# Taking chunks 8 to 15 through the first layers four at a time (512 columns) instead of two (256)

## The chip, the core and the metric

The program runs on one core of a Trainium2 chip. The metric is the device time of one execution in microseconds (us), as the median of several runs. Engines are named as in the profile: PE is the matmul engine (PEld its weight loads), DVE the vector engine, ACT the scalar engine, POOL the general one, SP the queue that issues most of the transfers.

## What is computed

Three stages follow one another on 3072 tokens (4 batches of 768) of 384 features (8 heads of 48):

```python
# 1: recurrent attention, one state of 48 x 48 per batch and head
cur = einsum('bhd,bhe->bhde', u * kt, vt)
y[t] = einsum('bhd,bhde->bhe', rt, state + cur)
state = wt[..., None] * state + einsum('bhd,bhe->bhde', kt, vt)
# 2: gated layers: w1, w2 are 384 x 1024, w3 1024 x 1024, w_out 1024 x 384
x2 = ((y @ w1) * (y @ w2)) @ w3 @ w_out
# 3: 8 experts, each token goes to its best two by a noisy gate on x2
out[token] += weight * (relu(x2 @ e1[e]) @ e2[e])
```

## The kernel before

**Precision.** Every large product is made of three matmuls (`mm3`, lines 181 to 184): an operand is held as a high part and a low part in a 32-bit format that the matmul takes, and high times high, high times low and low times high are summed in a PSUM bank. ACT writes the high part as a cast, DVE the low part as a subtraction.

**Stages.** First w3 and w_out are folded into one matrix of 1024 x 384, to which the 16 gate columns are joined (400 columns). Then attention and the first layers run interleaved over 24 chunks of 128 tokens (`NCH`), which make 12 groups of two (`NGRP`, counted from 0). Then come the 8 experts.

**First layers.** For group g the x of its two chunks (256 columns) lies in `xh` and `xl`. `mo_ab(g, fp, m)` (line 576) makes 256 of the 1024 features of y @ w1 (m = 0, bank `bA`) or y @ w2 (m = 1, bank `bB`): 18 matmuls of 256 columns. For m = 0 ACT copies the bank to `acs`; for m = 1 DVE multiplies `acs` by the bank into `pp`, ACT casts that to `ph`, and DVE makes `pl`. `mo_x(g, fp)` multiplies p by the folded matrix into the two banks `bX`, 12 matmuls of 400 columns, one step behind. At a group's end DVE copies the gate columns (`mo_lz`), and ACT copies the rest to `xos` and sends it off (`mo_out`).

**Attention of chunk j** goes through the steps in `STEPS`: DVE scans the decay (`pre_scan`, `fg`), ACT makes its reciprocal by Ln and Exp (`rc`), DVE refines it and forms the scaled keys and queries (`pre_rec`, `pre_k`, `pre_r`: `kt`, `rt`), POOL and DVE make the diagonal term (`rku`, `cc`), and ACT writes it in eight pieces into `am` (`pre_d`). PE makes the scores (`at_A`), DVE puts them into `am` (`at_ov`, two instructions), and PE makes y (`at_y`), from which ACT and DVE make `xh` and `xl`. For the state the scaled keys must be turned. From chunk 5 on ACT copies them to `kp` (`at_half`, a single buffer), a transfer from ACT's queue stores them in HBM (`key_halves`), and a transposing transfer from SP's queue brings them back as `kn` (`at_turn`). Then PE makes the new part of the state (`at_kv`), DVE scales it (`snew`) and ACT puts it into `S`.

**The order.** Each step has a slot; there are 12 slots to a group, and each slot holds one piece of the first layers, behind which the steps due are written. `WHEN` holds the slots of chunks 0 to 5 by hand; later chunks take `6 * j - 14 + LATE[i]`, so that one chunk of attention goes with six slots. The gate of four chunks (`gate_top`, `gate_put`) is placed by `gate_at`. DVE executes in the order in which the program is written from the start, PE from group 2 on, ACT only in the last group; before that a scheduler sets ACT's order, and SP's but for pinned transfers. Every engine takes its queue strictly in order.

Of the kernel before, what the change touches and what calls it, by code (L numbers as in the profile page):

```python
# [18 lines left out]
P = 128  # L19
# [5 lines left out]
NGRP = NCH // 2  # L25
# [28 lines left out]
ROWMAP = np.array([r for kb in PIECES for pc in kb for r in piece_rows(pc)])  # L54
TIMES = np.concatenate([np.arange(HC)[::-1], np.arange(HC, P)])
# [16 lines left out]
def tile_kernel(ctx: ExitStack, tc: tile.TileContext, dt, nat, w3t, wout, w1, w2, e1, e2, cf, ci, out):  # L72
# [61 lines left out]
    wp.tile([P, 48], F32, name="pad_w")  # L134
    W0 = [wp.tile([P, 4, XW], F32R, name=x) for x in ("W0h", "W0l")]
# [174 lines left out]
    def at_y(j):  # L310
# [189 lines left out]
    for k, slot in WLD.items():  # L500
        at(slot, load_w, *k)
    for i, fn in enumerate(STEPS):
        for j in range(NCH):
            late = 3 if j == NCH - 1 and i == 1 else 0
            at(WHEN[j][i] if j in WHEN else 6 * j - 14 + LATE[i] - late, fn, j)
# [92 lines left out]
    def low_p():  # L598

        while LOWP:  # L600
            l, p, h = LOWP.pop()
            dve.tensor_tensor(out=l, in0=p, in1=f(h), op=OP.subtract)
# [9 lines left out]
    def mo_lz(g):  # L612
        for tt in range(2):
            dve.tensor_copy(out=LZ[:, 2 * g + tt, :], in_=bX[tt][:, DM:XW])

    def mo_out(g, tts=(0, 1), pin=lambda x: x):
        for tt in tts:
            t = 2 * g + tt
# [635 lines left out]
```

## Time and profile before

| | |
|---|---|
| median of 3 runs | 883.08 us (882.89 to 884.78) |
| the profiled execution | 885.03 us, its span 883.2 us |
| mean granted clock of PE | 0.999 |
| busy share of PE, PEld, DVE, ACT, POOL | 98%, 92%, 56%, 49%, 28% |
| share of PE in the chain that ended last | 90% |

The span runs from the first to the last instruction; 1.8 us of the profiled execution lie outside it. The busy time of PE counts overlapped matmuls, so the pace of a stream of matmuls is read from the starts in a timeline. The chain that ended last is followed back from the last instruction, each step to what released it.

### The profile page before, as it was taken

The page shows a single profiled execution, that of the slowest core. Times are in us where ns is not written, and L with a number is a line of the kernel's source. Part 1 is how long each engine was busy: PE and PEld are TensorE (multiplying, and loading weights), DVE is VectorE, ACT ScalarE, POOL GpSimd, SP SyncE. Part 2 cuts the span into 40 slices and gives each one's busy share as a digit, 9 for nine tenths or more (in the row PEclk, how much of TensorE's full clock was granted, in tenths as well). Part 3 has the DMA queues.
Part 4 walks back from the last instruction along what each step waited for, and adds up shares of the span by engine and source line. Part 5 has one row for each costly group of instructions (what it writes and reads, how often), then busy time and mean ns, then how long its engine had stood idle before and what let it go on. Part 6 is the DMA issues. An engine that isn't in the chain of part 4 may idle for free.

```text
span 883.2 us, 18271 instructions
## 1 busy us (share of the span) xinstructions
PE 868.2 (98%) x7333; PEld 808.3 (92%) x7333; DVE 497.3 (56%) x1215; ACT 435.0 (49%) x876; POOL 243.9 (28%) x216
## 2 busy tenths in 40 slices
PE   8999999999999999999999999999999999999996
PEld 6789899999999999999999989899998998989896
DVE  6899875856756756765475453352534434343430
ACT  5777666566466456555454343433433344343431
POOL 2010021041141141232344343407052260613113
PEclk9999999999999999999999999999999999999999
DMA  9955399556467464433266587829368392854213
GB/s 348 390 207 208 97 128 264 134 172 191 118 202 186 133 177 128 98 120 122 69 190 130 157 252 200 210 59 239 84 181 186 93 217 63 242 121 102 27 13 48
DMA packets 123968, 139.22 MB, mean 158 GB/s; under 512 B 74977, under 2 KB 103649, under 8 KB 123873
## 3 DMA queue, kind: packets, MB, share of 16 engines
q1 hardware_dynamic: 100336, 109.58, 43.0%
q0 software_dynamic: 12160, 19.72, 11.6%
q10 hardware_dynamic: 11376, 8.65, 3.0%
q8 instruction: 59, 0.97, 0.5%
q14 instruction: 37, 0.30, 0.1%
HBM read 88.12 MB, written 36.04 MB: 141 GB/s over the span
## 4 chain that ended last, share of the span: by engine, by line
PE 90%; DVE 6%; ACT 2%; issue 1%; DMA 1%; POOL 0%; SPq 0%; POOLq 0%; DVEq 0%; ACTq 0%
PE pb L182 27%; PE pb L183 27%; PE pb L184 26%; PE pb L332 3%; PE pb L263 3%; PE pb L932 1%; PE pb L296 1%; DVE cvz L166 1%; DMA rawf<-wout 1%; DVE w3l L173 1%; ACT top L153 0%; DVE am L268 0%; DVE WAl L173 0%; DVE fg L210 0%; PE pb L412 0%
## 5 line engine op out<-in xcount | busy, mean ns | idle before, releaser
L937 POOL DMA_INDIRECT out<-ye,ti x49 | 76.7, 1565 | 225.3 <-ACT ye L927 204.8
L910 DVE SCALAR_TENSOR_TENSOR HH<-pb,HH 128x256 fp32r<-128x256 f32 (+1 forms) x128 | 71.1, 557 | 112.5 <-ACT HH L909 112.5
L182 PE MATMUL pb<-XTh,WAh 128*128 128x512 f32 (+1 forms) x384 | 131.7, 343 | 0.0
L184 PE MATMUL pb<-XTh,WAl 128*128 128x512 f32 (+1 forms) x384 | 131.4, 342 | 0.0
L183 PE MATMUL pb<-XTl,WAh 128*128 128x512 f32 (+1 forms) x384 | 131.0, 341 | 0.0
L182 PE MATMUL pb<-WBh,HH 128*128 128x384 f32 x384 | 129.3, 337 | 0.0
L184 PE MATMUL pb<-WBh,HH 128*128 128x384 f32 x384 | 128.4, 334 | 0.0
L183 PE MATMUL pb<-WBl,HH 128*128 128x384 f32 x384 | 128.4, 334 | 0.0
L909 ACT ACTIVATE HH<-pb 128x256 fp32r<-128x256 f32 (+1 forms) x128 | 62.7, 491 | 115.6 <-PE pb L184 113.4
L742 POOL DMA_INDIRECT slots<-g_sc,g_si x48 | 51.5, 1073 | 127.5 <-DVE g_si L741 71.9
L927 ACT ACTIVATE ye<-pb,ti 128x384 f32<-128x384 f32 x42 | 24.4, 582 | 124.2 <-PE pb L184 124.2
L183 PE MATMUL pb<-xl,WAh 128*128 128x256 f32 x288 | 80.9, 281 | 0.8 <-DVE xl L339 0.8
L182 PE MATMUL pb<-xh,WAh 128*128 128x256 f32 x288 | 81.5, 284 | 0.0
L183 PE MATMUL pb<-xl,WBh 128*128 128x256 f32 x288 | 81.1, 281 | 0.0
L182 PE MATMUL pb<-xh,WBh 128*128 128x256 f32 x288 | 81.0, 281 | 0.0
L184 PE MATMUL pb<-xh,WBl 128*128 128x256 f32 x288 | 81.0, 281 | 0.0
L184 PE MATMUL pb<-xh,WAl 128*128 128x256 f32 x288 | 80.8, 281 | 0.0
L183 PEld LDWEIGHTS pb<-XTl,WAh 128*128 128x128 f32 x384 | 72.3, 188 | 7.5
L184 PEld LDWEIGHTS pb<-XTh,WAl 128*128 128x128 f32 x384 | 72.2, 188 | 7.5
L182 PEld LDWEIGHTS pb<-XTh,WAh 128*128 128x128 f32 x384 | 72.0, 188 | 7.5
L182 PEld LDWEIGHTS pb<-WBh,HH 128*128 128x128 f32 x384 | 72.1, 188 | 5.0 <-ACT WAh L810 4.4
L243 POOL TENSOR_TENSOR rku<-nrk 128x384 f32<-128x384 f32 x21 | 21.3, 1012 | 196.5 <-DVE cc L250 80.8
(203 smaller groups left out, 2069.1 us busy)
## 6 DMA issues: line engine op xcount, KB each, us to landing
dtc<-dt SPq DMA_DIRECT2D x24, 772.0 KB, 5.1
raw<-e SPq DMA_DIRECT2D x18, 768.0 KB, 6.1
raww<-e SPq DMA_DIRECT2D x14, 768.0 KB, 5.0
nrk<-nat SPq DMA_DIRECT2D x24, 384.0 KB, 5.9
expert_rows<-xg SPq DMA_DIRECT2D x45, 192.0 KB, 4.4
rawf<-w3t SPq DMA_DIRECT2D x16, 512.0 KB, 7.2
nv<-nat SPq DMA_DIRECT2D x24, 256.0 KB, 4.5
out<-zeros SPq DMA_DIRECT2D x9, 576.0 KB, 3.7
```

The costliest lines, as they stand in the source:

```text
L166: dve.scalar_tensor_tensor(z, mid, 13, t, op0=OP.logical_shift_right, op1=OP.bitwise_or)
L182: pin(pe.matmul(o, wh, xh, start=start, stop=False))
L183: pe.matmul(o, wh, xl, start=False, stop=False)
L184: pe.matmul(o, wl, xh, start=False, stop=stop)
L243: on.tensor_tensor(out=t, in0=RK[j][:, :DM], in1=RK[j][:, DM:], op=OP.mult)
L263: pe.matmul(bST[hb][:, P * a:P * a + P], KT[j][q, a].rearrange("p s i -> p (s i)"), RT[j][q, a].rearrange("p s i -> p (s i)"), start=True, ...
L332: pe.matmul(o, lt, rh, start=st, stop=en, tile_position=tp)
L742: ins = pool.indirect_dma_start(out=table, out_offset=bass.IndirectOffsetOnAxis(ap=si[:, i, k:k + 1], axis=0), in_=SC[:, i, k, :], in_offs ...
L909: act.activation(out=Hh[hf][:, ff], in_=bank[:, :n], func=AF.Relu)
L910: dve.scalar_tensor_tensor(Hl[hf][:, ff], bank[:, :n], 0.0, f(Hh[hf][:, ff]), op0=OP.max, op1=OP.subtract)
L927: act.activation(out=y[:n], in_=bank[:n], func=AF.Copy, scale=wt)
L937: ins = pool.indirect_dma_start(out=out, out_offset=bass.IndirectOffsetOnAxis(ap=ti(e, j)[:, 0:1], axis=0), in_=y[:n], in_offset=None, com ...
```

## The change

Groups 4 and 5 now hold four chunks each (8 to 11 and 12 to 15), so there are 10 groups. In a group of four a `mo_ab` makes 128 features for 512 columns with 9 matmuls. p of two chunks goes straight through the second product (`mo_x4` with `tts` 0 and 1); p of the other two chunks is kept in `ps` (and `pl` for the last two features) and goes through it in a second pass, behind the first piece of the next group. Since a group of four needs four chunks of x at its start, the y of chunks 6 to 19 gets slots of its own (`YAT`): 26 instead of 28 for chunk 6, 34 instead of 40 for chunk 8, 46 instead of 58 for chunk 11, then falling back to the old pace by chunk 20. The other steps of a chunk are scaled by `f`, 4/6 where chunks follow one another by four slots. The buffers of x become one pair of tiles and one pair taken from the weight loader's pool; the gate of chunks 8 to 15 is placed later.

```diff
+GROUPS = ((0, 2, 0, 0), (2, 2, 0, 6 * P), (4, 2, 0, 0), (6, 2, 0, 6 * P), (8, 4, 1, 0), (12, 4, 0, 0),
+          (16, 2, 1, 0), (18, 2, 1, 6 * P), (20, 2, 0, 0), (22, 2, 0, 6 * P))
...
+    YAT = {4: 16, 5: 22, 6: 26, 7: 30, 8: 34, 9: 38, 10: 42, 11: 46, 12: 52, 13: 58, 14: 64, 15: 70, 16: 80, 17: 90,
+           18: 98, 19: 106}
+
+    def when(j, i):
+        if j in WHEN:
+            return WHEN[j][i]
+        base, y, f = 6 * j - 14, 6 * j - 8, 1
+        if j < 21:
+            base = YAT[j - 1]
+            y, f = YAT.get(j, y), min(1, (base - YAT[j - 2]) / 6)
+        return y - 3 * (j == NCH - 1 and i == 1) if LATE[i] == 6 else base + f * LATE[i]
...
-            at(WHEN[j][i] if j in WHEN else 6 * j - 14 + LATE[i] - late, fn, j)
+            at(when(j, i), fn, j)
...
+        if GROUPS[g][1] == 4:
+            for kb in range(3):
+                o = 768 * (fp // 2) + 256 * kb + P * (fp % 2)
+                mm3(bank, wh[:, o:o + P], wl[:, o:o + P], XH[g][:, kb], XL[g][:, kb], kb == 0, kb == 2)
...
+    def mo_p(g, fp):
+        p = PP[g, fp]
+        if GROUPS[g][1] == 4:
+            PF[g, fp] = [work.tile([P, 512], F32R, name="ph"),
+                         BP[0].tile([P, 512], F32R, name="ps", bufs=6) if fp < 6 else work.tile([P, 512], F32R, name="pl")]
+            for i, t in enumerate(PF[g, fp]):
+                act.copy(out=t[:, :256], in_=p[:, 256 * i:256 * i + 256])
+                LOWP.append((t[:, 256:], p[:, 256 * i:256 * i + 256], t[:, :256]))
...
+    def mo_x4(g, tts, ffs):
+        for tt in tts:
+            for ff in ffs:
+                t = PF[g, ff][tt // 2]
+                o = P * (tt % 2)
+                wh, wl = [W0[i][:, ff] if ff < 4 else W1[ff - 4][:, i] for i in range(2)]
+                mm3(bX[tt % 2][:, :XW], t[:, o:o + P], t[:, 256 + o:256 + o + P], wh, wl, ff == 0, ff == 7)
...
+        if four:
+            sub = [(mo_ab, g, 0, 0), None, (mo_ab, g, 0, 1)]
+            for ff in range(1, 8):
+                sub += [(mo_ab, g, ff, 0), (mo_ab, g, ff, 1), (mo_x4, g, (0, 1), (ff - 1,))]
+        if was:
+            sub = [x for x in sub if x]
+            sub[1:1] = [(mo_x4, g - 1, (0, 1), (7,))]
+            sub[3:3] = [(mo_x4, g - 1, (tt,), range(o, o + 4)) for tt in (2, 3) for o in (0, 4)]
```

On PE the new part of the state, y and the scores of the next chunk stand together. This is PE at chunk 6 before: the block (`nv,kn`, `am,nv`, `rt,kt`) follows the second piece of group 2 (`WB` names the weights w2).

```order
L182 MATMUL pb_73<-xh,WBh 128x256
L183 MATMUL pb_73<-xl,WBh 128x256
L184 MATMUL pb_73<-xh,WBl 128x256
L296 MATMUL pb_79<-nv,kn 32x48 x16
L332 MATMUL pb_76<-am,nv 32x128 x16
L263 MATMUL pb_77<-rt,kt 128x128
L263 MATMUL pb_78<-rt,kt 128x128
```

And now:

```order
L194 MATMUL pb_75<-w1p,ph 128x400
L195 MATMUL pb_75<-w1p,ph 128x400
L196 MATMUL pb_75<-w1p,pl 128x400
L308 MATMUL pb_79<-nv,kn 32x48 x16
L344 MATMUL pb_76<-am,nv 32x128 x16
L275 MATMUL pb_77<-rt,kt 128x128
L275 MATMUL pb_78<-rt,kt 128x128
```

The block has moved ahead by 36 matmuls of 256 columns: it now follows the last second product of group 1 (`w1p` is a part of the folded matrix).

This is ACT before, from the cast of chunk 5's x on (`acs` and the first `ph` belong to group 2's first piece, `kp` to chunk 7, the two `xos` to group 1):

```order
L338 CAST xh<-pb_76 128x3x128 [waits PE_49]
L222 ACTIVATE rc<-fg 128x512 [waits DVE_49]
L223 ACTIVATE rc<-rc 128x512 [waits Activation_49]
L586 COPY acs<-pb_72 128x512 [waits PE_49]
L595 CAST ph<-pp 128x512 [waits DVE_49]
L279 COPY kp<-kt 128x1024 [waits DMAHW3_49,DVE_49]
L620 COPY xos<-pb_74 128x768 [waits DMAHW2_49,DVE_49]
L620 COPY xos<-pb_75 128x768 [waits DVE_49]
L621 DMA x_rows<-xos 128x768 [waits DMAHW1_49,Activation_49]
```

And now:

```order
L348 CAST xh<-pb_76 128x3x128 [waits PE_49]
L234 ACTIVATE rc<-fg 128x512 [waits DVE_49]
L235 ACTIVATE rc<-rc 128x512 [waits Activation_49]
L291 COPY kp<-kt 128x1024 [waits DMAHW4_49,DVE_49]
L611 COPY acs<-pb_72 128x512 [waits PE_49]
L292 DMA key_halves<-kp 128x4x256 [waits DMAHW1_49,Activation_49]
L635 CAST ph<-pp 128x512 [waits DVE_49]
L268 ACTIVATE am<-cft,cc 128x128 [waits DVE_49]
L268 ACTIVATE am<-cft,cc 128x128 x7
L669 COPY xos<-pb_74 128x768 [waits DMAHW3_49,DVE_49]
L669 COPY xos<-pb_75 128x768 [waits DVE_49]
```

The copy of chunk 7's keys has moved ahead of group 2's first `acs`, and it now waits for a transfer's semaphore that the store of chunk 6's keys sets; the eight pieces of chunk 7's `am` stand ahead of `xos`.

This is DVE before, ahead of the product p of group 2's third piece (`pp`), the gate of chunks 0 to 3 being under way (`g_...`):

```order
L650 TENSOR_TENSOR g_l<-g_l,g_q 128x32 [waits DVE_49,Activation_49]
L651 TENSOR_TENSOR g_l<-g_l,cft 128x32 [waits DVE_49]
L652 TENSOR_TENSOR g_nl<-g_l,LZ 128x32 [waits DVE_49]
L226 TENSOR_TENSOR kt<-fg,rc 128x512 [waits Activation_49]
L227 SCALAR_TENSOR_TENSOR rc<-kt,rc 128x512 [waits DVE_49]
L656 MAX g_mx<-g_nl 128x8 x4
L658 MAX_INDEX g_mi<-g_mx,g_nl 128x8 [waits DVE_49] x4
L589 TENSOR_TENSOR pp<-acs,pb_73 128x512 [waits PE_49,Activation_49]
```

And now:

```order
L701 TENSOR_TENSOR g_nl<-g_l,LZ 128x32 [waits DVE_49]
L315 TENSOR_TENSOR stmp<-pb_79,snew 128x192 [waits PE_49]
L316 TENSOR_TENSOR snew<-stmp,sc 128x192 [waits DVE_49]
L349 TENSOR_TENSOR xl<-pb_76,xh 128x3x128 [waits Activation_49]
L222 SCALAR_TENSOR_TENSOR fg<-dtc,d_64 128x520 [waits DMAHW2_49]
L226 TENSOR_TENSOR sc<-fg 128x4 [waits DVE_49]
L705 MAX g_mx<-g_nl 128x8 x4
L707 MAX_INDEX g_mi<-g_mx,g_nl 128x8 [waits DVE_49] x4
L614 TENSOR_TENSOR pp<-acs,pb_73 128x512 [waits PE_49]
```

The low part of chunk 7's x (`xl`) and the scan of chunk 9 (`fg`) now stand ahead of that `pp`; before, nothing that waits for an x stood between chunk 6's x and it.

## Rows read from the trace of the kernel before

**Rows 1.** Busy time by stretch: engine, microseconds (instructions), then clock, DMA share, GB/s

```profile
147.00:190.00 43.00, 43.00 (x545) 41.46 (x544) 30.70 (x96) 27.12 (x61) 8.69 (x9) 1.00 0.60 176
```

**Rows 2.** Waits of PE, 111 to 420: total us, times, longest

```profile
PE pb L263 <- DVE rt L238: 0.3, 1, 0.3
```

**Rows 3.** Timeline of PE: start us, duration us, what

```profile
251.42 0.28 PE L182 MATMUL pb<-xh,WAh 128*128 128x256 f32 x1
...
255.68 0.35 PE L182 MATMUL pb<-W0h,ph 128*128 128x400 f32 x1
```

**Rows 4.** Timeline of PE, first layer of an expert

```profile
560.91 0.39 PE L182 MATMUL pb<-XTh,WAh 128*128 128x512 f32 x1
...
563.22 0.39 PE L183 MATMUL pb<-XTl,WAh 128*128 128x512 f32 x1
...
571.83 0.39 PE L182 MATMUL pb<-XTh,WAh 128*128 128x512 f32 x1
```

**Rows 5.** Timeline of PE, the product before the second group

```profile
145.69 0.34 PE L184 MATMUL pb<-w1p,pl 128*128 128x400 f32 x1
```

**Rows 6.** Chain of waits, 145 to 170: start us, us in the chain, what

```profile
150.28 0.48 PE pb L296 x32
...
152.72 0.39 PE pb L182
...
165.84 0.48 PE pb L296 x32
...
168.94 0.38 PE pb L182
```

**Rows 7.** Timeline of ACT, 126 to 162

```profile
129.97 1.05 ACT L279 COPY kp<-kt 128x1024 uint16<-128x1024 uint16 x1
...
146.29 1.49 ACT L620 COPY xos<-pb 128x768 uint16<-128x768 uint16 x2
...
148.69 0.59 ACT L586 COPY acs<-pb 128x512 f32<-128x512 f32 x1 [0.91 <-PE pb L184]
149.18 2.45 ACT L256 ACTIVATE am<-cft,cc 128x128 f32<-128x128 f32 x8
...
152.15 0.71 ACT L308 COPY S<-snew 48x192 f32<-48x192 f32 x2
152.89 0.48 ACT L338 CAST xh<-pb 128x384 fp32r<-128x384 f32 x1
...
155.91 1.28 ACT L644 ACT_TABLE_LOAD   x1
```

**Rows 8.** Timeline of SP, the turn of chunk 6's keys

```profile
144.07 1.26 SPq L284 DMA_TRANSPOSE kn<-key_halves  x1
```

**Rows 9.** DMA issues: what, KB each, median us to landing

```profile
key_halves<-kp ACTq DMA_DIRECT2D x15, 256.0 KB, 5.9
...
kn<-key_halves SPq DMA_TRANSPOSE x15, 3.6
```

**Rows 10.** Timeline of DVE, 126 to 162

```profile
139.11 1.36 DVE L268 COPY_PREDICATED am<-cit,pb 128x512 f32<-128x512 int32 x2
...
141.07 0.69 DVE L227 SCALAR_TENSOR_TENSOR rc<-kt,rc 128x512 f32<-128x512 f32 x1
...
144.56 0.42 DVE L231 TENSOR_TENSOR kt<-dtc,fg 128x256 f32<-128x256 f32 x1
...
147.43 0.55 DVE L250 TENSOR_REDUCE cc<-rku 128x8 f32<-128x384 f32 x1
...
153.40 0.56 DVE L339 TENSOR_TENSOR xl<-pb,xh 128x384 fp32r<-128x384 f32 x1 [2.06 <-ACT xh L338]
153.88 1.23 DVE L210 TENSOR_TENSOR_SCAN fg<-dtc,d 128x520 f32<-128x520 f32 x1
...
159.76 0.37 DVE L656 MAX8 g_mx<-g_nl 128x8 f32<-128x8 f32 x4
...
160.59 0.67 DVE L589 TENSOR_TENSOR pp<-acs,pb 128x512 f32<-128x512 f32 x1
```

More of the change, by code (lines that the diff above doesn't have):

```diff
@@ L24 @@
 CPB = S // P
-NGRP = NCH // 2
+NGRP = 10
 HC = P // 2
@@ L600, in low_p @@
         while LOWP:
-            l, p, h = LOWP.pop()
+            l, p, h = LOWP.pop(0)
             dve.tensor_tensor(out=l, in0=p, in1=f(h), op=OP.subtract)
@@ L610, in mo_x, with mo_lz @@
                 mm3(bX[tt][:, :XW], PH[g, fp][:, s], PL[g, fp][:, s], wh, wl, ff == 0, ff == 7)
-    def mo_lz(g):
-        for tt in range(2):
-            dve.tensor_copy(out=LZ[:, 2 * g + tt, :], in_=bX[tt][:, DM:XW])
+    def mo_x4(g, tts, ffs):
[5 more added lines that the diff above has]
+                mm3(bX[tt % 2][:, :XW], t[:, o:o + P], t[:, 256 + o:256 + o + P], wh, wl, ff == 0, ff == 7)
+    def mo_lz(g, tts=(0, 1)):
+        for tt in tts:
+            dve.tensor_copy(out=LZ[:, GROUPS[g][0] + tt, :], in_=bX[tt % 2][:, DM:XW])
     def mo_out(g, tts=(0, 1), pin=lambda x: x):
         for tt in tts:
-            t = 2 * g + tt
+            t = GROUPS[g][0] + tt
+            tt = tt % 2
             xo = xos[:, 2 * DM * tt:2 * DM * tt + 2 * DM]
@@ L1003, in tile_kernel @@
                          (5, store_first, 0), (5, store_first, 1), (6, gather_first, 2, NCH - 2 * GB), (8, store_first, 2)):
-        at(SPG * (NGRP - 2) + slot, fn, *a)
+        at(SPG * (NCH // 2 - 2) + slot, fn, *a)
+    BP = []
+    bigx = ExitStack()
     for g in range(NGRP):
+        c0, four = GROUPS[g][0], GROUPS[g][1] == 4
+        was = g > 0 and GROUPS[g - 1][1] == 4
         if g == 2:
@@ L1010, in tile_kernel @@
             ctx.enter_context(tc.manual_schedule(engines={mybir.EngineType.Activation}))
+        if four and not BP:
+            cvx.close()
+            BP.append(bigx.enter_context(tc.tile_pool(name="bigp", bufs=1)))
+            BP[0].tile([P, 56], F32, name="pad_p")
         sub = [(mo_ab, g, 0, 0), (mo_ab, g, 0, 1), None, (mo_ab, g, 1, 0), (mo_ab, g, 1, 1), (mo_x, g, 0),
@@ L1021, in tile_kernel @@
             load_e(0, 0, 1)
-        for i in range(12):
+        cost = [.5 if x and x[0] == mo_x4 and len(x[2]) == 2 else 1 for x in sub]
+        first_slot, slots = SPG * c0 // 2, SPG * GROUPS[g][1] // 2
+        edges = [first_slot - .5 + slots * sum(cost[:n]) / sum(cost) for n in range(len(sub) + 1)]
+        for i in range(len(sub)):
             if sub[i]:
@@ L1026, in tile_kernel @@
                 fn(*a)
+                if fn == mo_x4 and a[0] < g:
+                    if a[2][-1] == 7:
+                        mo_lz(a[0], a[1])
+                        mo_out(a[0], a[1])
+                    if a[1] == (3,) and a[2][-1] == 7:
+                        mo_p(g, 0)
             elif g:
@@ L1030, in tile_kernel @@
                 mo_out(g - 1)
-            k = SPG * g + i
-            run_todo(k - .5, k)
-            if i not in (1, 4, 7, 10 if g < NGRP - 1 else 9):
+            lo, hi = edges[i:i + 2]
+            mid = (lo + hi) / 2
+            run_todo(lo, mid)
+            if not (sub[i] and sub[i][0] == mo_ab and sub[i][3] == 1) if four or was else i not in (
+                    1, 4, 7, 10 if g < NGRP - 1 else 9):
                 low_p()
-            run_todo(k, k + .5)
+            run_todo(mid, hi)
             act.on = False
```

32 lines of the change are left out of this document (21 added, 11 removed).

## The prediction, made before the change was timed

> **What bounds the kernel now.** I read the busy time by stretch first, then what PE waits for, then PE's timeline. In the stretch where the change acts PE is busy all the time at its full clock (the granted share is 1.00), DVE 71% and ACT 63% of it [rows 1]. From 111 to 420 us PE waits once for another engine, for 0.3 us [rows 2]. So what shortens PE's own work shortens the kernel by as much, and every wait that the change gives PE is paid in full. Both sides of the sum are therefore on PE.
>
> **What the wider matmul saves.** A matmul's price is the distance to the next start, as they overlap. From 251.42 to 255.68 us stand 36 matmuls of 256 columns: 118.3 ns each [rows 3]. An expert's first layer runs the same three products at 512 columns: 48 of them from 560.91 to 571.83, 227.5 ns each [rows 4]. At 2.4 GHz, the upper of the clock's levels, 256 columns alone are 106.7 ns and 512 are 213.3, so each instruction carries 12 to 14 ns beyond its columns, whatever its width. The first products of chunks 8 to 15 were 4 groups x 4 x 2 pieces x 18 = 576 matmuls of 256; now they are 2 groups x 8 x 2 pieces x 9 = 288 of 512. Each saves 2 x 118.3 - 227.5 = 9.2 ns: **2.65 us less**. The first ten go at 231 ns, with other engines busy [rows 4]; at that pace the saving is 5.6 ns each, 1.6 us, the lower bound. I take 2.65 since 38 of the 48 go at 226 to 227.
>
> The Trainium skill (page "TensorE: Matmul & The Clock Gate", section "Back-to-back issue gap") gives a warm matmul N / 2.4 + 2.5 ns. By that the saving would be 2.5 ns each, 0.7 us, as an estimate, and the total below some 1.9 us higher; the trace shows 118.3 ns where it gives 109.2 [rows 3], and the trace decides.
>
> **What costs nothing.** The 192 matmuls of 400 columns of these groups stay, only in another order. Each product p is now cast and subtracted in two halves: 16 instructions more on ACT and on DVE, hidden while those are ahead of PE. Between two fillings of a bank by y @ w1 or y @ w2 there were 36 x 0.118 / 2 + 12 x 0.18 = 4.3 us in which ACT had to empty it; now 9 x 0.2275 + 6 x 0.18 = 3.1 us. Copies of 0.6 us [rows 7] fit, unless ACT is inside the eight pieces of `am`, 2.45 us; I take 0, with 1 us as the upper bound. A zero fill of the output that SP now issues earlier falls where DVE sets the pace: 0.
>
> **What the earlier attention costs.** Chunks 6 to 11 now follow one another by four slots, not six. Two new waits come of it, and a third behind them. I work them out on PE's clock of the profiled execution; up to 139 us PE, DVE and ACT have the same order in both.
>
> *The state of chunk 6.* The block of state, y and scores of chunk 6 has moved ahead by 36 matmuls, behind the second product that ends at 145.69 + 0.18 [rows 5]; with some 0.2 us for the change of shape (an estimate) it wants to begin at 146.1. It needs the turned keys. SP issued their transpose at 144.07, when the store had landed [rows 8], and such a transpose lands 3.6 us later [rows 9]: 147.7. Neither store nor turn has moved. **Wait: 1.6 us.** If they land 2 us sooner it is 0; a store 2 us later makes it 3.6.
>
> *The third piece of group 2.* In ACT's new order the copy of chunk 7's keys needs the single buffer that the store of chunk 6 frees at about 144.0 [rows 8], and group 2's first `acs` stands behind it. From there I follow the two queues to the product that frees bank `bB`. Durations are those of ACT [rows 7] and of DVE [rows 10]:
> - kp 1.05, acs 0.59, product 0.67, two queries 0.84, cc 0.55: 3.70
> - ACT: am of chunk 7 2.45, two xos 1.49, S 0.71, x high 0.48: 5.13
> - DVE: x low 0.56, scan of chunk 8 1.23, am 1.36, two of the reciprocal 1.38, product 0.67: 5.20
> - ACT: cast of p as acs 0.59, two table loads of the gate 2.56, kp 1.05, am 2.45, acs 0.59, S 0.71, x high of chunk 7 0.48: 8.43
> - DVE: x low 0.56, scan of chunk 9 1.23, the gate's search 0.83 (159.76 to 160.59 [rows 10]), product 0.67: 3.29
>
> This sums to 25.75; with 0.6 for the gate's logarithm and the issue of a store on ACT (my estimate, the size of a small row) the bank is free at 144.0 + 26.35 = 170.35. PE without any wait would want it at 167.0: from 145.87 a block of 2.44 (150.28 to 152.72 [rows 6]), 36 matmuls 4.26, 12 of 400 columns 2.19, 18 for 2.13, a block with a state 3.10 (165.84 to 168.94 [rows 6]), 18 for 2.13, 12 for 2.19, 18 for 2.13, and 0.6 for the changes of shape. With the wait above that is 168.6. **Wait: 1.75 us.** If the engines overlap their instructions by 0.1 us each, as the 0.42 us steps do (the one at 144.56 stands for several [rows 10]), the chain is some 2 us shorter and this wait is 0; if every handover between engines costs 0.1 us more, it is 3.
>
> *The scores of chunk 9.* Behind that product DVE still has, before chunk 9's queries are ready, am 1.36, nine small gate steps (1.0, estimated from four in 0.37 [rows 10]), the reciprocal 1.38, a low part 0.67, keys and queries 1.68: 6.1 us. PE has 2.13 of matmuls, then the state and y, some 2.2: 4.35. **Wait: 1.75 us**, between 0 and 3 by the same overlaps.
>
> Behind it DVE gains on PE again: counting its instructions from one chunk's `xl` to the next in the new order, by the durations of [rows 10], it has 8 to 9 us of work for each of chunks 10 to 12, and PE 11.7 to 13.6.
>
> **The sum.** -2.65 + 1.6 + 1.75 + 1.75 = +2.45 us. Against the profiled execution's 885.03 us (its span of 883.2 and 1.8 around it) this gives 887.5; that execution lies 1.95 above the median of the runs, 883.08, and so I expect a median of **885.5 us**, slower by 0.28%.
>
> **The rivals.**
> - *No new wait* (faster). The queues overlap enough for DVE to keep ahead, and chunk 6's keys land by 146. For it: before the change DVE waits for ACT's cast of x (2.06 us [rows 10]) and so has time in hand. Against: the chain above has 3.3 us too much for PE's slack without a wait. It decides at the bank: if that product ends before 167 us of the old clock, nothing is lost. Then the whole saving stands, 880.4 us.
> - *One wait of the three.* Only the keys are late, or DVE's lag is taken up by the keys' wait before it. 883.08 - 2.65 + 1.6 = 882.0; with half of another 883.
> - *The keys of chunks 8 and 9 come late too.* Their chain of copy, store (5.9 us) and turn (3.6) [rows 9] has 15.6 us from copy to use at four slots of about 2.9 us, and ACT's copy is late behind the table loads; I find each in time by less than 1 us. Missed by 1.5 us each: 888.5.
> - *The wide matmul saves little,* because near the busy engines it goes at the 231 ns of the first ten [rows 4]: 886.5 with my waits. By the Trainium skill's formula above (same page and section) it would be 887.4, an estimate. That the program does not do what it says I exclude: PE's new order holds 288 matmuls of 512 columns where 576 of 256 stood.
>
> **How the numbers follow.** Chances: my three waits 0.42, no new wait 0.27, one of them 0.18, late keys beyond that 0.10, little saving 0.03. What a measurement of this kernel can tell from no change is about 0.2%, 1.8 us: faster means below 881.3, slower above 884.9. My own case, 885.5 give or take 1.5, lies above in two thirds or more and in the middle otherwise. Faster 0.28 (the first rival and a little of the second), same 0.32, slower 0.40. The range for 8 in 10 goes from the first rival, 880.4, to the late keys with some of the 1 us at the banks, 889.0; since both signs are in it: my case alone is 884.0 to 887.5.
>
> **What would show it.** In the new profile: 288 rows of 512 columns at 227 ns from start to start (231 would mean the smaller saving); in PE's waits a line of the state's matmuls behind `kn` at about 147 us, one of the group's matmuls behind the product of DVE near 169, one of the scores behind `rt` near 175. If PE's waits from 111 to 420 us stay under 0.5 us, the chain of 26 us is wrong, and the time is about 880.4. If there are waits in groups 4 and 5 instead, the 3.1 us between two fillings of a bank were too few. The time from 430 us to the end must not change in length; if it does, the gate's later slots have moved the experts.

## Result and the profile after

The change makes the kernel slower by 1.4%: the forecast's direction, nearly five times its size (1.35% for 0.28%), and outside its range.

| | before | after |
|---|---|---|
| median | 883.03 us (6 runs, 882.66 to 884.78) | 894.52 us (6 runs, 892.72 to 900.86) |
| ratio | | 1.0135 (1.0103 to 1.0167) |
| profiled execution, its span | 885.03, 883.2 us | 892.97, 891.2 us |
| mean granted clock of PE | 0.999 | 0.996 |
| busy share of PE, DVE, ACT, POOL | 98%, 56%, 49%, 28% | 98%, 57%, 49%, 28% |
| start of chunk 6's scores | 136.04 us | 134.20 us |
| first matmul of the experts | 455.59 us | 463.70 us |

Behind the first expert matmul both take 420.0 us to the last one. So the loss lies between 134 and 464 us, and there it is 9.95 us, as the profiled execution of after was 1.8 us ahead at its start. (It was the second fastest of its six; before's lay 2.0 above its median.)

PE's waits from 111 to 420 us in the changed kernel (total us, times, longest); before there was one of 0.3 us [rows 2]:

```profile
PE pb L194 <- DVE pp L614: 2.1, 1, 2.1
PE pb L308 <- DMA kn<-key_halves: 1.4, 1, 1.4
PE pb L275 <- DVE rt L250: 1.1, 4, 0.5
PE pb L196 <- DVE pl L642: 0.7, 1, 0.7
PE pb L194 <- ACT xrh L348: 0.6, 1, 0.6
PE pb L344 <- issue: 0.5, 2, 0.3
```

The first two are waits of the prediction, near their size. The third adds up four chunks, at 159, 175, 199 and 241 us; chunk 9, to which the prediction's third wait belongs, has 0.20 of it, at 175.14. The view counts from the modelled end of the matmul before; by the distances between starts the gaps are longer and sum to some 8.5 us. Busy time by stretch, changed kernel (engine busy us, instructions; then clock, DMA share, GB/s):

```profile
147.00:190.00 43.00, 40.45 (x537) 38.06 (x538) 34.56 (x95) 28.62 (x63) 9.01 (x9) 0.96 0.63 178
...
160.00:169.80 9.80, 7.71 (x60) 7.22 (x57) 6.79 (x24) 7.45 (x18) 2.02 (x2) 1.00 0.69 201
169.80:173.20 3.40, 3.40 (x46) 3.18 (x49) 3.16 (x13) 0.34 (x1) 0.00 (x0) 0.50 0.02 5
173.20:180.00 6.80, 6.60 (x114) 6.04 (x104) 6.73 (x15) 5.57 (x15) 2.04 (x2) 1.00 0.61 186
```

The first row answers to [rows 1]: PE was busy for all of 43 us, now 40.45, and DVE rose from 30.70 to 34.56. The new thing is the clock. Behind the wait for `pp` it stands at 0.50 (1.2 GHz) for 3.4 us, for which the prediction had no term. PE's timeline shows it in the matmuls' starts (start us, us, what):

```profile
166.69 0.27 PE L196 MATMUL pb<-xh,WAl 128*128 128x256 f32 x1
169.06 0.39 PE L194 MATMUL pb<-xh,WBh 128*128 128x256 f32 x1 [2.09 <-DVE pp L614]
...
169.63 0.28 PE L195 MATMUL pb<-xl,WBh 128*128 128x256 f32 x1
169.75 0.35 PE L196 MATMUL pb<-xh,WBl 128*128 128x256 f32 x1
169.89 0.42 PE L194 MATMUL pb<-xh,WBh 128*128 128x256 f32 x1
170.10 0.42 PE L195 MATMUL pb<-xl,WBh 128*128 128x256 f32 x1
...
172.24 0.41 PE L196 MATMUL pb<-xh,WBl 128*128 128x256 f32 x1
```

2.37 us after the last start the next one comes; 0.8 us later the distance goes from 0.12 to 0.21 us (eleven of them from 169.89 to 172.24, 0.214 each), where [rows 3] have 0.118. So 45% of the 3.4 us is lost, 1.5 us. The Trainium skill (page "TensorE: Matmul & The Clock Gate", section "What's actually happening") says that the clock follows how busy PE has been of late; this row agrees.

The chain that the prediction walked to this `pp` can be followed on ACT and DVE:

```profile
142.24 1.05 ACT L291 COPY kp<-kt 128x1024 uint16<-128x1024 uint16 x1 [4.35 <-DMA key_halves<-kp]
...
157.54 1.28 ACT L689 ACT_TABLE_LOAD   x1
...
165.18 0.48 ACT L348 CAST xh<-pb 128x384 fp32r<-128x384 f32 x1
```

```profile
151.71 0.56 DVE L349 TENSOR_TENSOR xl<-pb,xh 128x384 fp32r<-128x384 f32 x1 [5.07 <-ACT xh L348]
...
165.69 0.56 DVE L349 TENSOR_TENSOR xl<-pb,xh 128x384 fp32r<-128x384 f32 x1 [2.88 <-ACT xh L348]
166.16 1.23 DVE L222 TENSOR_TENSOR_SCAN fg<-dtc,d 128x520 f32<-128x520 f32 x1
...
168.34 0.67 DVE L614 TENSOR_TENSOR pp<-acs,pb 128x512 f32<-128x512 f32 x1
```

From the store's landing at 142.2 to the end of `pp` at 169.0 it took 26.8 us, 26.35 forecast. DVE isn't short of time: it stood still twice, 5.07 and 2.88 us, for an x that ACT had behind other work, with `pp` queued behind it. ACT, in turn, worked with no gap over 0.2 us from 156.90 to 165.66, the gate's two table loads among its work. So what makes `pp` late is DVE's place in line behind ACT's queue, not DVE's own load.

PE at the start of group 4, where the prediction had nothing:

```profile
214.06 0.35 PE L196 MATMUL pb<-w1p,pl 128*128 128x400 f32 x1
215.01 0.49 PE L194 MATMUL pb<-xrh,WAh 128*128 128x512 f32 x1 [0.60 <-ACT xrh L348]
215.60 0.50 PE L195 MATMUL pb<-xrl,WAh 128*128 128x512 f32 x1
215.94 0.40 PE L196 MATMUL pb<-xrh,WAl 128*128 128x512 f32 x1
...
217.33 0.40 PE L196 MATMUL pb<-xrh,WAl 128*128 128x512 f32 x1
...
218.79 0.45 PE L196 MATMUL pb<-w1p,pl 128*128 128x400 f32 x1 [0.69 <-DVE pl L642]
```

Chunk 11's x comes 0.6 us late (ACT writes chunk 12's `am` first, 2.45 us), its low part and a `pl` follow late. And the wide matmul's price can be read: six distances from 215.94 to 217.33, 231.7 ns each, not the 227.5 of the experts [rows 4]. Over both groups of four, the waits left out, the mean is 232.6.

### The profile page after: what moved, and what is told of

Its sections match the earlier page's. It is cut to its first block, busy times and chain, and to the rows that moved or that the text cites. A ratio compares the mean times of both kernels' runs of the same rounds, so it can differ in the third digit from the quotient of the medians.

```text
span 891.2 us, 17731 instructions
## 1 busy us (share of the span) xinstructions
PE 870.8 (98%) x7045; PEld 794.0 (89%) x7045; DVE 507.0 (57%) x1231; ACT 436.5 (49%) x892; POOL 246.7 (28%) x216
## 4 chain that ended last, share of the span: by engine, by line
PE 74%; DVE 13%; ACT 6%; DMA 3%; issue 2%; ACTq 0%; POOL 0%; SPq 0%; POOLq 0%; DVEq 0%
PE pb L194 23%; PE pb L195 23%; PE pb L196 23%; ACT am L268 2%; PE pb L344 2%; DMA rawf<-wout 2%; DVE am L280 2%; DVE fg L222 2%; DMA key_halves<-kp 1%; PE pb L275 1%; PE pb L981 1%; DVE rc L239 1%; DVE pp L614 1%; DVE kt L238 1%; DVE cvz L178 1%
## 5 line engine op out<-in xcount | busy, mean ns | idle before, releaser
L255 POOL TENSOR_TENSOR rku<-nrk 128x384 f32<-128x384 f32 x21 | 23.5, 1117 | 245.6 <-DVE cc L262 121.4
L194 PEld LDWEIGHTS pb<-WBh,HH 128*128 128x128 f32 x384 | 72.1, 188 | 5.0 <-ACT WAh L859 3.8
L862 DVE TENSOR_TENSOR WAl<-raww,WAh 128x768 fp32r<-128x768 f32 x28 | 26.7, 958 | 85.8 <-ACT WAh L859 65.5
L195 PEld LDWEIGHTS pb<-WBl,HH 128*128 128x128 f32 x384 | 72.1, 188 | 0.0
L196 PEld LDWEIGHTS pb<-WBh,HH 128*128 128x128 f32 x384 | 72.1, 188 | 0.0
L268 ACT ACTIVATE am<-cft,cc 128x128 f32<-128x128 f32 x176 | 55.0, 390 | 6.5 <-DVE cc L262 5.8
L923 POOL DMA_INDIRECT xg<-x_rows,ti x45 | 46.5, 1033 | 33.5 <-DMA ti<-slots 17.7
L614 DVE TENSOR_TENSOR pp<-acs,pb 128x512 f32<-128x512 f32 x48 | 32.7, 682 | 37.7 <-PE pb L196 27.2
```

The source lines that it names most:

```text
L194: pin(pe.matmul(o, wh, xh, start=start, stop=False))
L195: pe.matmul(o, wh, xl, start=False, stop=False)
L196: pe.matmul(o, wl, xh, start=False, stop=stop)
L268: act.activation(out=AM[j][:, h], in_=ident, func=AF.Copy, scale=KS["c", j][:, h:h + 1])
L862: dve.tensor_tensor(out=l, in0=src, in1=f(h), op=OP.subtract)
L923: pool.indirect_dma_start(out=XG[e, j][:rows_of(j)], out_offset=None, in_=x2d[:rows], in_offset=bass.IndirectOffsetOnAxis(ap=ti(e, j)[:, 0 ...
```

## The experiments

Differences are to the kernel before, run on the same chip in the same session (medians 883.6 to 884.9). The change itself (+11.5) was timed in another session. Views show one execution, which lies up to 2.2 us off its run's median; so the text sometimes gives the loss of that execution between chunk 6's scores and the first expert matmul, beside the 319.55 us of before (the change: 9.95).

| run | difference, us | ratio, 95% |
|---|---|---|
| early attention alone (e1) | +8.4 | 1.0062 to 1.0135 |
| wide groups alone (e2) | +1.3 | 0.9998 to 1.0028 |
| second `kp` (e3) | +8.7 | 1.0061 to 1.0120 |
| late gate (e4) | +12.3 | 1.0107 to 1.0166 |
| PE turns chunk 6 (e5) | +7.2 | 1.0062 to 1.0096 |
| before, one block moved (e6) | +4.5 | 1.0037 to 1.0070 |
| e1 with PE's turn (e7) | +4.5 | 1.0036 to 1.0069 |
| e1 with a filler (e8) | +9.1 | 1.0088 to 1.0122 |
| e7 with the late gate (e9) | +2.1 | 1.0010 to 1.0037 |
| even pace, groups of two (e10) | +10.8 | 1.0104 to 1.0135 |
| even pace, groups of four (e11) | +8.6 | 1.0086 to 1.0117 |
| e6 with a filler (e12) | +3.0 | 1.0021 to 1.0046 |
| change, PE's turn, late gate (e13) | +12.7 | 1.0123 to 1.0155 |
| e11, gates placed (e14) | +1.6 | 1.0005 to 1.0032 |
| e10, gates placed (e15) | +3.2 | 1.0022 to 1.0044 |
| change without `rku` (e16) | +16.7 | 1.0168 to 1.0196 |
| e5 without `rku` (e17) | +17.6 | 1.0176 to 1.0223 |
| e2 without `rku` (e18) | +11.0 | 1.0103 to 1.0143 |

### The two halves apart

Theory 1 puts the loss on the early attention, theory 2 on the groups of four.

```diff
-NGRP = 10
+NGRP = 12
...
-GROUPS = ((0, 2, 0, 0), (2, 2, 0, 6 * P), (4, 2, 0, 0), (6, 2, 0, 6 * P), (8, 4, 1, 0), (12, 4, 0, 0),
-          (16, 2, 1, 0), (18, 2, 1, 6 * P), (20, 2, 0, 0), (22, 2, 0, 6 * P))
+GROUPS = ((0, 2, 0, 0), (2, 2, 0, 6 * P), (4, 2, 0, 0), (6, 2, 0, 6 * P), (8, 2, 1, 0), (10, 2, 1, 6 * P),
+          (12, 2, 0, 0), (14, 2, 0, 6 * P), (16, 2, 1, 0), (18, 2, 1, 6 * P), (20, 2, 0, 0), (22, 2, 0, 6 * P))
...
```

> Twelve groups of two as before the change, with the attention's new slots and the gate's new slots kept: the early attention alone. Theory 1 (early attention): ACT and DVE can't keep a chunk in four slots beside the gate, and PE waits for them; nearly the whole loss stays, and the saving of the wide matmuls (some 1.2 us at the 232 ns of the changed kernel's trace) is missing: 892 to 897 us, with PE's waits for kn and for pp near 144 and 167 us of 1.4 and 2.1 us as in the changed kernel. Theory 2 (groups of four): the loss comes from the wide groups, their 3.1 us between two fillings of a bank and their start that needs four chunks of x: 882.5 to 886 us. Half and half, 888 to 890, would mean that both count.

```diff
+                rd = vs[1 if c in (16, 18) else 0]
+                wr = vs[1 if 8 <= j < 20 else 0]
...
-        if j < 21:
-            base = YAT[j - 1]
-            y, f = YAT.get(j, y), min(1, (base - YAT[j - 2]) / 6)
```

> Groups 4 and 5 of four chunks as in the change, but every y at its old slot, 6 j - 8. The x of chunks 8 to 15 comes too late for that, so groups 4 and 5 read the x of chunks 4 to 7 in its place (the output is not the reference's); all instructions stay, in number and size. Theory 1 (early attention): no wait is left, only the wide matmuls' saving: 881.9 at 232 ns a matmul, 880.4 at 227.5; range 880 to 883.5. Theory 2 (groups of four): most of the loss is still there, 890 to 894, with PE's waits inside groups 4 and 5, for bA, bB or bX.

Early alone: 892.9 us, +8.4, some 3 of the 11.5 short. Wide alone: 885.8, +1.3, where -1.1 to -2.7 was due; PE waited there 0.6 us for a `pp` and 0.2 for an x. So the early attention makes most of the loss, and the wide groups gain nothing where they stand (the waits seen there don't make up all of what is missing). PE's waits and the clock of the early attention alone:

```profile
PE pb L308 <- DMA kn<-key_halves: 2.1, 1, 2.1
PE pb L275 <- DVE rt L250: 1.7, 1, 1.7
```

```profile
143.20:146.80 3.60, 1.47 (x63) 1.17 (x65) 2.93 (x8) 2.33 (x7) 1.20 (x1) 1.00 0.84 189
146.90:153.70 6.80, 6.80 (x45) 6.40 (x38) 2.52 (x5) 4.02 (x10) 1.25 (x2) 0.50 1.03 233
```

Here the wait for `kn` is 2.1 us, and 6.8 us at half clock follow. They cost 3.0 us: from the state's first matmul to the 22nd of the next first products it takes 8.06 us, and 5.02 in e8 below, which has the same order and full clock there. With the wait for `rt`, 1.7, that is 6.8 of the 8.2 that this execution loses in the stretch.

### The price of the first wait

> The kernel before with one move: the block of state and y of chunk 6 at slot 26 in place of 28, as the change has it. This prices the first wait alone. PE should wait for kn near 146 us, by 1.4 to 2.9 us as in the runs of the changed kernels. Theory 1a (a wait of over 2 us brings the clock down for 3.4 or 6.8 us): slower than before by 1.4 to 2.9 where the clock stays, by 3.8 to 6.3 where it falls; 886 to 890 beside 884. Rival, the prediction's own step: the wait costs its length alone, 885.5 to 886.5. If DVE and ACT gain from the earlier x and PE waits less behind it (there was one wait of 0.3 us), nothing is given back.

```diff
-at(WHEN[j][i] if j in WHEN else 6 * j - 14 + LATE[i] - late, fn, j)
+at(WHEN[j][i] if j in WHEN else 26 if j == 6 and LATE[i] == 6 else 6 * j - 14 + LATE[i] - late, fn, j)
```

> The kernel before with the block of chunk 6 at slot 26 (889.06: a wait for kn of 2.3 us and 3.4 us at half clock), and nine matmuls of 400 columns (1.65 us, their result unused) ahead of the state of chunk 6. Nothing is late behind that block, so the fall of the clock stands by itself here: if it comes from PE standing still, the wait shrinks to some 0.7 us, the granted clock stays at 1.00, and 1.7 us come back: 887 to 887.7. If it falls all the same: 889.

```diff
     def do_kv(j):
+        if j == 6:
+            for _ in range(9):
+                pe.matmul(bY[:, :XW], W0[0][:, 0, :P], W0[0][:, 1], start=True, stop=True)
```

PE's wait and the clock around it with the block moved alone (e6), and then with the filler (e12):

```profile
147.65 0.87 PE L296 MATMUL pb<-nv,kn 128*32 128x48 f32 x32 [2.32 <-DMA kn<-key_halves]
...
150.91 0.28 PE L182 MATMUL pb<-xh,WAh 128*128 128x256 f32 x1
```

```profile
147.50:150.80 3.30, 3.15 (x67) 2.79 (x68) 0.36 (x2) 1.18 (x3) 0.00 (x0) 0.50 0.30 106
```

```profile
147.75 0.54 PE L296 MATMUL pb<-nv,kn 128*32 128x48 f32 x31 [0.86 <-DMA kn<-key_halves]
...
149.56 0.28 PE L182 MATMUL pb<-xh,WAh 128*128 128x256 f32 x1
```

```profile
147.50:150.80 3.30, 3.05 (x78) 2.88 (x79) 1.16 (x3) 1.18 (x3) 0.00 (x0) 1.00 0.56 170
```

This pair is the clearest of the study. The second row of each is the fourth matmul of the next first products: the same work takes 3.26 us in e6 and 1.81 in e12, so the half clock costs 1.45. One block moved ahead costs 4.5 us; its profile shows 2.3 of waiting and these 1.45. With idle work put into the wait, nothing comes sooner, yet the clock holds and 1.4 us come back (889.06 to 887.65, 1.7 expected). The clock's fall is a cost of standing still, beside the wait itself.

### Taking the late keys away

> The change with chunk 6's keys turned by PE (four transposes into bY and one copy on ACT), as chunks 0 to 4 do it, in place of copy, store and turn. Theory 1a: a wait of PE of some 2 us or more costs its length and, behind it, a stretch of 3.4 or 6.8 us at the granted clock of 0.5, 1.7 or 3.4 us more. The wait for kn near 144 us and its fall go, and chunk 7's copy no longer waits for a store; what is left is the late rt of chunk 9 (some 2 us) and the start of group 4 (2 us): 887 to 890 beside 884 of before. Rival: ACT and DVE are late in any case by the sum of their work, and the time lost at kn comes back at the next wait: 892 to 895.

> The early attention with twelve groups of two, and chunk 6's keys turned by PE. Beside the early attention alone (892.9, with a wait for kn of 2.1 us, 6.8 us at half clock behind it and a wait for rt of 1.7): theory 1a expects both the wait and the fall gone, 886 to 889; the rival (lag of ACT and DVE comes back at the next wait) 891 to 893.

```diff
-    JT = 5
+    JT = 7
```

> The early attention with twelve groups of two, and nine matmuls of 400 columns (1.65 us, their result unused) ahead of the state of chunk 6, so that PE works through most of its wait for kn. No wait of an engine is shorter: what is late stays late. If the fall of the clock comes from the wait and costs what the rows say, it is gone: 1.7 to 3.4 us less than the early attention alone (892.9), 889.5 to 891, with the granted clock at 1.00 from 140 to 160 us. If the fall has another cause, or is only a matter of the records: 892.5 to 895.

The line shown is all of e5's edit; e7 adds it to the edit of e1, and e8 adds the filler of e12 to the edit of e1.

e7 came out at 889.1 (+4.5, 3.8 less than e1), between the two expectations; the clock stays at 1.00, and PE waits:

```profile
PE pb L194 <- DVE pp L614: 1.8, 1, 1.8
PE pb L275 <- DVE rt L250: 1.7, 1, 1.7
```

These are the prediction's second and third wait at its 1.75 us each. In e1 the first was hidden: PE had lost 5.1 us at `kn` and came late to the bank. The filler of e8 shows the other side: the wait for `kn` fell to 1.0 with no half clock behind it, but PE, sooner by that, waited 2.1 us for `pp`, with 3.4 us of half clock behind that, and 1.2 for the gate's `g_rb`, and nothing was gained (893.7). The rival in e5's expectation holds in part: lag that one wait hides comes out at the next. e5, with groups of four, came out between its two ranges too, at 891.8 (+7.2 instead of +11.5), and stays 2.7 above e7.

### What makes ACT and DVE late

> The change with a second buffer for kp (even chunks use xgs, which is idle until the experts), so that chunk 7's copy on ACT need not wait for the store of chunk 6. By the prediction's chain the copy then starts some 4.3 us sooner, at 138 us, all that stands behind it on ACT follows sooner, and the product that frees bB near 167 us is no longer late: the 2.1 us wait goes, and with it the granted clock of 0.5 that followed it for 3.4 us: 3 to 4 us less, 890 to 892. The wait for kn near 144 us stays at 1.5 us, since the store and the turn of chunk 6 don't move. If the chain is not what holds the product, the time stays at 894.5 and the wait is still 2 us.

```diff
-        kp = att.tile([P, 4, 2, P], U16, name="kp", bufs=1)
+        kp = xgs[:, :8 * P].rearrange("p (a t s) -> p a t s", a=4, t=2)
+        if j % 2:
+            kp = att.tile([P, 4, 2, P], U16, name="kp", bufs=1)
```

> The change with the gate of chunks 0 to 3 moved from slot 27 to slot 47, behind the chunks that follow by four slots, and that of chunks 4 to 7 from 51 to 64. If the gate inside the dense stretch (two table loads of 1.28 us on ACT, some 4 us of small steps on DVE) is what makes the chain too long, PE's waits near 167, 175 us are gone and the clock stays at 1.00 there: 890 to 891.5, the wait for kn and those near 199 to 218 us staying. If they only move to 198 to 220 us, where the gate now stands: 894 to 897.

```diff
-gate_at(SPG * ((t0 + GB) // 2) + {8: 7.5, 12: 5.5}.get(t0, 3), t0, 1 + late,
+gate_at({0: 47, 4: 64}.get(t0, SPG * ((t0 + GB) // 2) + {8: 7.5, 12: 5.5}.get(t0, 3)), t0, 1 + late,
...
```

Neither decided: in both `kn` came 2.9 us late, with half clock behind it, which covers any lag at `pp`, and e4 met a new wait of 2.2 us for the gate's `g_rb`, with a fall of 3.4 us behind it. So the gate was moved where the keys were repaired:

> The early attention with twelve groups of two and chunk 6's keys turned by PE (889.1, PE waiting 1.8 us for pp and 1.7 for rt near 165 and 171 us), with the gate of chunks 0 to 3 moved from slot 27 to 47 and that of chunks 4 to 7 from 51 to 64. If the gate inside the dense stretch makes the chain too long (two table loads of 1.28 us and the small steps on DVE), both waits go: 885 to 886. If four slots a chunk are too few for ACT and DVE even without the gate, both waits stay within 0.5 us: 888.5 to 890. A wait for g_rb near 185 to 240 us, where the gate now stands, would add 1 to 4.

886.8, just above the 885 to 886 expected and 2.4 less than e7, and PE's waits from 111 to 420 us shrink to

```profile
PE pb L308 <- issue: 0.9, 2, 0.5
PE pb L344 <- issue: 0.2, 1, 0.2
```

Both waits are gone: four slots a chunk are enough for ACT and DVE, but not with a gate among them. For groups of two, then, late keys and the gate explain the early attention's loss but for 2.1 us, of which this profile shows 1.1.

> The change whole, with both repairs: chunk 6's keys turned by PE, and the gate of chunks 0 to 3 behind the dense stretch (slot 50.5, that of chunks 4 to 7 at 62.5), so placed that its bank bK is read four slots before the next chunk's state needs it. If the late keys, the gate in the dense stretch and the clock behind them are all of the loss: 884 to 886.5 beside 884.6, since the repaired attention with groups of two gave 886.8 and the wide matmuls save some 1 us. If groups of four cost time of their own (PE waiting at their start for x, in them for pp and pl): 887 to 889.5.

```diff
-gate_at(SPG * ((t0 + GB) // 2) + {8: 7.5, 12: 5.5}.get(t0, 3), t0, 1 + late,
+gate_at({0: 50.5, 4: 62.5}.get(t0, SPG * ((t0 + GB) // 2) + {8: 7.5, 12: 5.5}.get(t0, 3)), t0, 1 + late,
...
+    JT = 7
```

A plain miss: 896.3, worse than the change. In groups of four the gate is no better placed behind the dense stretch:

```profile
PE pb L196 <- DVE ph L642: 3.7, 2, 3.5
PE pb L194 <- DVE pp L614: 1.7, 1, 1.7
```

The low part of p, `ph`, stood behind an `xl` for which DVE waited 3.66 us on ACT, and PE, whose second product follows its p by one piece, waited 3.5, with 3.4 us of half clock behind it.

### Where nothing has to hurry

The even pace starts from chunk 6's old slot and reaches chunk 15 at slot 70; the groups of four are chunks 12 to 19.

```diff
+    YAT = {4: 16, 5: 22, **{j: 28 + 14 * (j - 6) / 3 for j in range(6, 16)}, 16: 76, 17: 82, 18: 88, 19: 94,
+           20: 104, 21: 112, 22: 121}
...
+          (12, 4, 0, 0), (16, 4, 1, 0), (20, 2, 0, 0), (22, 2, 0, 6 * P))
```

> Twelve groups of two, with chunks 6 to 15 following one another by 4.67 slots from the old slot 28 on (chunk 15 at slot 70 instead of 82), keys turned by transfers as before, the change's gate slots kept. If the four slots a chunk and the block moved ahead of its keys were what cost time, PE waits for nothing over 0.5 us: 884 to 886, beside 884.5 of before. If any attention that runs ahead makes ACT and DVE late, there are waits for rt or pp of 1 us and more: 887 to 890.

> The same even pace of 4.67 slots, with groups of four for chunks 12 to 15 and 16 to 19. The wide matmuls save 288 x (2 x 118.5 - 233) = 1.1 us. If the waits that the groups of four brought with the early attention (for pl, pp, rt and x high at their start, 0.4 to 0.9 us each, some 3 us) came from the lag of ACT and DVE: 1 us less than the same pace with groups of two. If they belong to groups of four: 0.5 to 2 us more than it.

Both missed for a reason of their own, the bank `bK`, which the gate and the state share (e10):

```profile
PE pb L308 <- DVE g_rb L761: 5.3, 2, 3.3
```

```profile
173.40:176.10 2.70, 0.32 (x3) 0.12 (x2) 2.63 (x13) 1.74 (x3) 0.37 (x1) 1.00 0.06 17
176.20:186.30 10.10, 9.28 (x114) 8.39 (x115) 5.23 (x13) 5.90 (x15) 2.69 (x3) 0.50 0.99 249
```

A chunk's state now fell right behind a gate's matmul into `bK`, which DVE had not read yet. With the 3.3 us came 10.2 us of half clock, 0.9 of them still in the wait; at 45% the rest is some 4.2 us lost. With the gates put right behind a state instead:

> Groups of four for chunks 12 to 15 and 16 to 19 at the even pace of 4.67 slots, as before, but the gates placed so that bK is read four slots before the next state, which takes away the two waits for g_rb (3.1 and 2.0 us) and the half clock behind them. If nothing else waits, the saving of the wide matmuls, some 1 us, is left: 883 to 884.5, no slower than the kernel before. If groups of four bring waits of their own: 885 to 887.5.

```diff
+        gate_at({0: 29.43, 4: 52.77, 8: 75, 12: 104.1, 16: 125.5}[t0], t0, 2 if late else steps,
```

> The same even pace and the same gates with twelve groups of two: the control for the run above. Expected 884 to 886, PE waiting for nothing over 0.5 us. The run above minus this one is the worth of the wide matmuls: about 1 us less if they save what their pace says, zero or more if groups of four give it back.

885.2 and 886.7: the first lies in the range for waits of their own, the second 0.7 above its range. Groups of four are 1.5 us faster than the same pace with groups of two, about the 1.1 expected, but the two intervals overlap; between the two profiled executions it is 0.8 in the stretch. So a small saving of the wide matmul fits, and these runs don't prove it. This pace costs groups of two 3.2 us (PE waits 0.7 us for `xos` in it, 0.9 in e14). No version beat the kernel before.

### POOL beside DVE

> The change, with POOL's two instructions for the diagonal term left out from chunk 6 on (cc is made from chunk 5's rku, so the output is not the reference's); the order on PE, DVE and ACT is the same to the row. In the changed kernel 14 instructions of DVE between 111 and 420 us are stretched from 0.2 to 0.7 us to 0.8 to 2.0 while POOL works on rku, 9.6 us in all; before the change it was two, 0.6 us. Theory 3: DVE stands still for POOL there, and PE's waits behind DVE (pp, rt, pl) shrink with it: 2 to 4 us less than the change, +7.5 to +9.5 on the kernel before, with the wait for kn left. If the stretched ones fall where DVE waits for ACT's x anyway (2.9 us at 165 us): +10.5 to +12 as the change.

> The change with chunk 6's keys turned by PE (+7.2 on the kernel before), and POOL's rku left out from chunk 6 on as above. The wait for kn is out of the way here. Theory 3: the waits for pp, rt and those in the groups of four (7 us in all) lose 2 to 4: +3 to +5. If not: +6.5 to +7.5.

> Groups of four at the old pace (+1.3 on the kernel before, output not the reference's), and POOL's rku left out from chunk 6 on. In that run 11 instructions of DVE were stretched, 7.1 us in all, and PE waited 0.7 us for pp and 0.4 for x low. Theory 3: these waits go and the wide matmuls' saving shows: -1.2 to 0. If groups of four cost it by themselves: +0.8 to +1.5.

```diff
     def pre_u(j):
+        if j > 5:
+            KS["u", j] = KS["u", 5]
+            return
```

All three missed by 5 to 10 us, because the edit did more than was meant. SP no longer waited for POOL to free a buffer and issued its `nrk` loads sooner, ahead of the keys' turn (e16):

```profile
144.64 2.63 SPq L207 DMA_DIRECT2D nrk<-nat  x2
...
147.84 1.26 SPq L299 DMA_TRANSPOSE kn<-key_halves  x1
```

PE waited 7.0 us for `kn` in e16 and 4.6 in e18 (in e17, where PE turns those keys, 5.1 for an `acs` of ACT and 3.9 for a `pl`; why, was not followed), and each had 10.2 us of half clock with it. The question itself is answered away from there: in e18 the waits for `pp` near 308 us and for `xrl` near 352 have the size that they had in e2 (gaps of 0.74 and 0.42 us in both), and in e17 those in group 4 for `pl` and `rt` (0.85 and 0.65 us) that of e5 (0.87 and 0.66), with POOL's work gone. Theory 3 is not borne out at these four places. For the `pp` near 169 us the changed kernel's trace speaks against it: the stretched rows ahead of it stand at 160 to 162 us (shown at the end), and DVE then stood still for 2.88 us until ACT, which had other work all that time, gave it chunk 7's x. In one place it does hold. In e10 the row of DVE ahead of the `g_rb` for which PE waited 3.3 us was stretched:

```profile
175.75 0.99 DVE L759 TENSOR_TENSOR g_b<-g_ct,cft 128x8 f32<-128x8 f32 x1
176.78 0.19 DVE L761 TENSOR_TENSOR g_rb<-pb,g_b 128x32 f32<-128x32 f32 x1
```

Elsewhere in that run the same row takes 0.15 us at its shortest; POOL worked on `rku` from 175.73 to 176.72. So some 0.8 us of that wait is POOL's, and as much of the second one, of 2.0 us near 252, where the row stands at 0.99 again.

## Why the prediction was wrong, point by point

Three of its steps failed: that a wait costs its length alone (half clock behind it added 1.5 us), that groups of four bring no waits of their own (some 2 to 3 us), and the size of the wide matmul's saving (1.2 us for 2.65).

- *What bounds the kernel.* Right: PE paid every wait, and the experts kept their length. That a wait is paid at its length alone was not (see below).
- *The wide matmul, -2.65 us.* Mis-sized. In this stretch it goes at 232.6 ns, so 288 x (236.6 - 232.6) = 1.2 us; e14 against e15 gives 0.8 to 1.5, not clear of the noise. The row of the first ten, taken as the lower bound at 231 ns [rows 4], was the nearer one. The reason given for it, other engines busy, holds for POOL alone (1.79 of 2.40 us); while those ten ran, DVE did nothing and ACT 0.69 us (behind the length stand PE, PEld, DVE, ACT and POOL):

```profile
560.90:563.30 2.40, 2.40 (x12) 1.97 (x12) 0.00 (x0) 0.69 (x2) 1.79 (x3) 1.00 1.09 319
```

Why a wide matmul goes at 227 ns in one place and at 232 in another stays open.

- *State of chunk 6, 1.6 us.* Mechanism and place right: 1.4 us in the profile, 2.1 to 2.9 in e1, e3, e4 and e6; no later keys kept PE waiting. The step that failed is that a wait costs its length: moved alone, in e6, it cost 4.5 us, with 2.3 of waiting and 1.45 of half clock in the profile.
- *Third piece of group 2, 1.75 us.* Right: 2.1 us, a chain of 26.8 us for 26.35. Again the clock came on top, 1.5 us.
- *Scores of chunk 9, 1.75 us.* Right in size where PE was at full clock (1.7 us in e1, e5 and e7). In the changed kernel PE was at half clock just then and came late itself; chunk 9's scores waited 0.20 us there.
- *"What costs nothing".* Wrong. Groups of four wait at their start and in them (x high 0.6, `pl` 0.7, further `rt`), about 3 us over groups of two (+11.5 against e1's +8.4, from two sessions whose intervals overlap; e5's +7.2 against e7's +4.5, from one session and clear; in the stretch of the profiled executions 1.7 and 3.3). It took in the banks alone, not that four chunks' x and p must pass ACT and DVE in time.
- *"DVE gains on PE again".* Wrong for the same reason. DVE's work per chunk was counted rightly, but not that it stands still in its queue for ACT's x while work that PE needs lies behind it.
- *The clock.* The sum took 1.00 throughout. In the profiled execution the fall costs 1.5 us, in e1 3.0, in e10 some 4.2. By the rows of the changed kernel 1.2 us are saved, the gaps sum to 8.5 and the clock costs 1.5: 8.8 of the 9.95 us that its execution lost. The sum had 2.65, 5.1 and nothing for these.

What stays open: why `kn` lands up to 1.5 us apart between runs, the 1 to 2 us by which e9 and e15 lie above what their waits show, and the median's further 3.5 us over the profiled execution's difference. Longer falls in the other runs don't explain these alone: the run with the highest mean clock, 0.999, took 894.67 us, more than the profiled one with 0.996.

## What to carry to other kernels

Where PE is always busy, price a new wait of some 2 us at its length and, as a risk, a stretch of half clock behind it, 1.5 to 4 us here, and look for what PE can do in it. Work moved ahead of the chain that feeds it gains nothing until the chain moves too: follow copy, store and turn, then each queue that they stand in. And a saving of a few ns per matmul is no firmer than the spread of its price over the kernel's stretches: take the slower row for the forecast.

## What the runs showed of the hardware that was not expected

**The clock falls quickly.** From 111 us to the experts, falls to 0.50 came behind, or within, every wait of PE of 2.2 us and longer (2.2 in e4, 2.3 in e6, 2.9 in e3 and e4, 3.1 in e11, 3.3 in e10, 3.5 in e13, 3.9 to 7.0 in e16 to e18), and three of 2.1 (e1, e8 and the change). They lasted 3.4, 6.8 or 10.2 us. Of the shorter waits, one of 1.7 in e16 had a fall 1.5 us after its end; the others of 1.7 and 1.8, one of 2.0 in e10 and in e11 each, and one of 2.1 in e5 had none. e11 has a fall near 199 us without a long wait, behind the small matmuls of an attention block that came with gaps. And in four of the twenty profiles (e6, e13, e14, e16) the clock fell for 3.4 us near 32 us, ahead of all that the edits touch, behind a wait of 0.9 us and matmuls of 16 columns that stand in the other profiles too. So the length of the wait alone doesn't settle it.

**DVE can stand still for POOL.** Two rows of DVE in the changed kernel, and POOL's at that time:

```profile
159.99 1.00 DVE L699 TENSOR_TENSOR g_l<-g_l,g_q 128x32 f32<-128x32 f32 x1
161.03 0.19 DVE L700 TENSOR_TENSOR g_l<-g_l,cft 128x32 f32<-128x32 f32 x1
161.25 0.90 DVE L701 TENSOR_TENSOR g_nl<-g_l,LZ 128x32 f32<-128x32 f32 x1
```

```profile
159.56 1.39 POOL L255 TENSOR_TENSOR rku<-nrk 128x384 f32<-128x384 f32 x1 [11.23 <-DVE cc L262]
161.02 1.08 POOL L256 TENSOR_TENSOR rku<-rku,cft 128x384 f32<-128x384 f32 x1
```

The same operation takes 0.19 or 1.00 us; the long ones end with POOL's (160.95 and 162.10). From 111 to 420 us 14 such two-input instructions of DVE (TENSOR_TENSOR) were stretched, by some 10 us in all over the shortest of their kind; before the change two, by 0.6. From 147 to 190 us four of them and a scan make some 4 us, as much as DVE's rise from 30.70 to 34.56. The Trainium skill (page "SBUF — State Buffer", section "SBUF: two separate sides") has DVE operations with two SBUF inputs and a GpSimd operation that reads SBUF shut each other out for a whole instruction; these rows agree.
